# Fillers and a piecewise loop in the first transform, and new steps for pieces of batches one and two, in an FFT filter fused with a two-layer network

## The chip, the cores and the metric

The kernel runs on one core of one Trainium2 chip. The metric is device time in microseconds (us), the median of several executions. Every profile shown is one execution taken by the hardware profiler. In it PE is TensorE's matmul row, PEld its weight loads, DVE is VectorE, ACT is ScalarE, POOL is GpSimd and SP is SyncE; a "q" behind an engine's name means its sequencer or its DMA queue.

## The reference

```python
X = np.fft.rfft(x, axis=1)                  # x: (8, 3008, 256)
F = (filt_r + 1j * filt_i)[None, :, :]      # (1505, 256)
y = np.fft.irfft(X * F, n=3008, axis=1)     # global filter per channel
h = y.reshape(24064, 256) @ w_in            # (256, 2048)
g = np.maximum(h, 0) + alpha * np.minimum(h, 0)
out = g @ w_out                             # (2048, 256)
```

Eight batches are filtered along the sequence in the frequency domain, and each filtered row goes through a two-layer network with a leaky activation (one slope for each hidden unit).

## The kernel before

All matmuls are in fp16 with fp32 sums in PSUM. The order of all work is written out by hand: each engine executes its instructions in the order in which the program issues them.

**The transform.** A length of 3008 is 94 x 32. One transform has four stages. `piece_a` is the transform over the 94 (eight pieces). Its result is turned, so that the 32 lie on partitions: for batches 1 to 7 through memory (`save_a` writes `a_dram`, `turn_a` reads it back, both from SP's queue), for batch 0 on TensorE (`turn_at`, a matmul against the identity `id16`). `piece_b` is the transform over the 32 for some frequencies, into PSUM; VectorE multiplies what it gives by the filter (lines 186, 187, and 301 for batch 0). `piece_c` goes back over the 32, `keep_c` or an eviction stores it as `v`, and it is turned again (`turn_c` with `v_dram` and `zt`; for batch 0 `half_t` and `piece_t` on TensorE). The last stage, `half_d` or `pair_d`, goes back over the 94 and evicts into `yT`, the network's input.

**The first transform** (batch 0, class `First`) stands ahead of everything else. Until its first quarter is in `yT`, the network can't start. Its loop over `kp` (12 pairs of frequencies) runs two `piece_b`, two `piece_c`, one `keep_c` on ScalarE for both and one `turn_at`. In its waits `warm(n, kind)` puts n fillers: matmuls of `id16` against a broadcast of itself, 512 columns each, whose results nobody reads.

**The network** is cut into 48 blocks of 512 or 384 rows, and each block into 16 steps. In a step `up(j)` makes 128 hidden units of the block (two matmuls, line 457, into `hps`; ScalarE and VectorE activate into `gtb`), and `down(j)` does a sixteenth of the second layer of the block before (line 488, into `op`). A step has a number from 0 to 767. The transforms of batches 1 to 7 run as pieces put at fixed steps, by `plan_fft(b, a_at, ta, quarters, x_at, b_at, add, c_at, d_at)`: steps of the eight `piece_a`, of `turn_a`, of the loads of the next batch's x, of the six `piece_b`, `piece_c` and the eight `pair_d`.

**PSUM** has eight banks: `psH` two tiles of two banks (`hps`: `up`, `piece_a`, `piece_c`, and `piece_b` of batch 0), `psO` two tiles of one bank (`op`: `down`, fillers, `piece_c` of batch 0), and `psF` a single tile of two banks. `psF` is shared by `piece_b` of batches 1 to 7, whose tile VectorE reads twice, and by `pair_d`, whose tile ScalarE reads once. Whoever comes next on `psF` waits until the readers of the one before are done.

The code around the change, as it was:

Of the kernel before, what the change touches and what calls it, by code (L numbers as in the profile page):

```python
# [50 lines left out]
def kernel(  # L51
# [57 lines left out]
    def load_x(b, c):  # L109
        xs = p_x.tile([N1, 8 * D], FP16, name="xs")  # L110
        for r in (slice(0, 48), slice(48, N1)) :
            nc.gpsimd.dma_start(out=xs[r], in_=xrow(b, c)[r])  # L112
        return xs
# [13 lines left out]
    def banks(wide):  # L127
        if wide:
            return psH.tile([128, 2, 512], FP32, name="hps")
        return psF.tile([128, 2, 512], FP32, name="psF")  # L130

    def bank(kind):
        if kind == "o":
            return psO.tile([128, 2, D], FP32, name="op").rearrange("p k d -> p (k d)")
        return banks(kind == "h")[:, 0]


    class Fft:
# [61 lines left out]
        def piece_c(self, q):  # L200
            if q == 0:
                self.v = p_fft.tile([128, NK, D], FP16, name="v")
                self.zt = p_fft.tile([96, N2, D], FP16, name="zt")
            u, _ = self.uw.pop(q)
            ps = psH.tile([128, 2, 512], FP32, name="hps")
            for h in range(2):
                for e in range(2):
                    r = slice(64 * e, 64 * e + 64)
                    for par in range(2):
                        nc.tensor.matmul(ps[64 * par : 64 * par + 64, e, 256 * h : 256 * h + 256],  # L210
                                         twi_s[r, 4 * q + 2 * h + par], u[r, par, h], start=True, stop=True)
            on_act(self.v[:, 4 * q : 4 * q + 4].rearrange("p (h e) d -> p e h d", e=2),
                   ps.rearrange("p e (h d) -> p e h d", h=2))
# [19 lines left out]
                                 wi3_s, start=True, stop=True)  # L233
            return ps

        def half_d(self, i, evict, kind):
            g, dh, mh = i // 4, (i // 2) % 2, i % 2
            ps = self.inverse(bank(kind), g, dh, mh)
            t0 = self.base + g * NX
            evict(yT[:, dh, t0 : t0 + NX].rearrange("p (x m) -> p x m", m=8)[:, :, 4 * mh : 4 * mh + 4],  # L240
                  ps.rearrange("p m x -> p x m"))
# [16 lines left out]
    both = (on_act, on_dve)  # L258


    class First(Fft):
# [42 lines left out]
        def piece_c(self, kp):  # L304
            if kp % 2 == 0:
                self.ops = [psO.tile([128, 2, D], FP32, name="op") for _ in range(2)]
            u = self.uw.pop(kp)
            tw, tx = (t.rearrange("p k (c g e) -> p k g c e", c=2, e=4) for t in (twi_s, twx_s))
            for par in range(2):
                for f in range(2):  # L310
                    for i, t in enumerate((tw, tx)):
                        for e in range(2):
                            r = slice(64 * e, 64 * e + 64)
                            o = self.ops[e][:, kp % 2].rearrange("p (g w) -> p g w", g=16)
                            o = o[:, 8 * f : 8 * f + 8, 8 * par : 8 * par + 8]
                            nc.tensor.matmul(o.rearrange("p g (c e) -> p g c e", c=2),  # L316
                                             u[r, par, i, 128 * f : 128 * f + 128], t[r, 2 * kp + par],
                                             start=(i == 0), stop=(i == 1))

        def keep_c(self, kp, evicts):  # L320
            vm = self.vm.rearrange("p (g q k e) -> p g q k e", q=4, k=NK, e=4)
            for e in range(2):
                k = 2 * kp + e
                evicts[e](vm[:, :, :, k : k + 3 : 2], self.ops[e].rearrange("p k (g q e) -> p g q k e", q=4, e=4))

        def turn(self, pt, i, n):
            m = self.vm.rearrange("p (g m e) -> p g m e", m=96, e=4)
# [20 lines left out]
    def tables(eng, names, ka, kb):  # L348
        for n, t in (("twf", twf_s), ("twi", twi_s), ("twx", twx_s)):
            if n in names:  # L350
                eng.dma_start(out=t[:, ka:kb], in_=consts[n].ap()[:, ka:kb])

    xc = {(0, c): load_x(0, c) for c in range(4)}
    f0 = First()
# [14 lines left out]
    for c in range(4):  # L369
        xc[(1, c)] = load_x(1, c)  # L370

    def warm(n, kind="o"):
        pw = bank(kind)
        for _ in range(n):
            nc.tensor.matmul(pw.rearrange("p (r c) -> p r c", r=4), id16,
                             id16.unsqueeze(1).to_broadcast([128, 4, 128]), start=True, stop=True)

    warm(9)
    for i in range(8):
        f0.piece_a(i, both[i % 2], i % 3 < 2)  # L380
        if i % 2 == 1:
            warm((4, 2, 2, 2)[i // 2])
        if i == 5:
            nc.vector.memset(twf_s[:, 8:24, 0:1], 0.0)
            tables(nc.sync, ("twf", "twi", "twx"), 8, 24)
            nc.sync.dma_start(out=wi3_s, in_=consts["wi3"].ap())
            nc.sync.dma_start(out=wf1_s, in_=consts["wf1"].ap())
            nc.sync.dma_start(out=sgn_s, in_=sgn_d.ap())
            alp = psO.tile([128, 2, D], FP32, name="op")
            nc.tensor.transpose(alp[:, 0, 0:16], al16, id32)  # L390
            nc.vector.tensor_copy(al_s, alp[:, 0, 0:16])
            nc.vector.tensor_scalar(alm_s, al_s, 1.0, -1.0, OP.mult, OP.add)
    f0.turn_at(0, 1, on_act)
    f0.turn_at(1, 1, on_dve, True)
    f0.piece_b(0)
    f0.turn_at(2, 2, on_act)
    f0.piece_b(1)
    f0.turn_at(4, 2, on_act)
    for kp in range(0, 12, 2):
        if kp < 10:  # L400
            f0.piece_b(kp + 2)
            f0.piece_b(kp + 3)
        f0.piece_c(kp)
        f0.piece_c(kp + 1)
        f0.keep_c(kp, both if kp == 10 else (on_act, on_act))
        if kp < 6:
            f0.turn_at(kp + 6, 2, on_act)
        elif kp < 10:
            warm(1, "f")
    nc.gpsimd.dma_start(out=filt_s[:, 0:1], in_=f0.fst)  # L410
    for o in range(0, 128, 64):
        for i in range(0, 64, 32):
            nc.gpsimd.dma_start(out=filts_s[o + i : o + i + 32], in_=filt_s[o + 32 : o + 64])
    for o in (32, 96):
        nc.gpsimd.dma_start(out=filt_s[o : o + 32], in_=filt_s[o - 32 : o])
    warm(2, "f")
    for i, (evict, kind) in enumerate(((on_act, "o"), (on_dve, "o"), (on_act, "f"), (on_dve, "h"))):
        f0.half_t(i, evict, kind)
    warm(4)
    for i, evict, kind in ((0, on_act, "h"), (2, on_dve, "o"), (1, on_act, "o"), (3, on_dve, "f")):  # L420
        f0.half_d(i, evict, kind)


    sizes = [512] * 5 + [384] + [512] * 6
# [74 lines left out]
    def put(step, fn, *args):  # L499
        plan.setdefault(step, []).append((fn, args))  # L500

    def plan_fft(b, a_at, ta, quarters, x_at, b_at, add, c_at, d_at):
        f = Fft(b)
        for i in range(8):
            put(a_at[i], f.piece_a, i)
            front.add(a_at[i])
        for c in range(4):
            put(a_at[2 * c + 1], f.save_a, c)
            if b + 1 < NB:
                put(x_at[c],  # L510
                    lambda b=b, c=c: xc.update({(b + 1, c): load_x(b + 1, c)}))
        for q in range(quarters):
            w = NK // quarters
            put(ta, f.turn_a, nc.sync, w * q, w * q + w)
        for q in range(6):
            put(b_at[q], f.piece_b, q, not add)
            if add:
                put(b_at[q] + add, f.piece_s, q)
        for q in range(6):
            put(c_at[q], f.piece_c, q)  # L520
            front.add(c_at[q])
            if q % 2 == 1:
                put(c_at[q] + 1, f.turn_c, q // 2)
        for i in range(8):
            put(d_at[i], f.pair_d, i, on_act)
# [15 lines left out]
    def d_steps(p):  # L541
        return [p + t for t in (91, 93, 104, 108, 116, 120, 140, 152)]

    plan_fft(1, range(12, 28, 2), 28, 4, (17, 21, 25, 29), range(36, 72, 6), 0, range(48, 84, 6),
             (91, 93, 98, 101, 106, 116, 136, 152))
    plan_fft(2, (50, 56, 62, 68, 74, 80, 84, 88), 92, 4, (57, 69, 81, 89), (104, 114, 126, 136, 148, 158), 7,
             (114, 126, 136, 148, 158, 170), d_steps(96))
    for b in range(3, NB):
        p = 96 * (b - 1)
# [54 lines left out]
```

## Time and profile before

| | us |
|---|---|
| median of 3 executions | 793.56 (792.51 to 794.36) |
| profiled execution: time | 792.9 |
| profiled execution: span, first to last instruction | 791.1 |
| TensorE busy in the span | 768.3 (97%) |
| VectorE, ScalarE, GpSimd busy | 596.7, 582.9, 142.9 |
| mean granted TensorE clock | 0.989 of full speed |
| first matmul of step 0 | at 42.09 |

How to read the rows below: times are from the start of the span. A row of the timeline has the start, the time from the first to the last of its instructions, engine, line, operation, tile written and tiles read, shape, count, and in brackets how long the engine had been idle and what ended that. A row of the windows has the stretch, its length, busy time and count of each engine (PE, PEld, DVE, ACT, POOL), the granted TensorE clock, the mean share of DMA engines in use and GB/s. A matmul's record lasts longer than the time that it keeps the next one from starting: 273 ns for 256 columns of line 488, where the next starts 109 ns later.

### The profile page before, as it was taken

How to read it: one execution, taken by the hardware profiler on the slowest of the kernel's cores; microseconds unless marked ns; L12 is line 12 of the kernel's file. 1: busy time of each engine (PE TensorE's matmuls, PEld its weight loads, DVE VectorE, ACT ScalarE, POOL GpSimd, SP SyncE). 2: the span in 40 equal slices, each digit the busy share in tenths (PEclk: the TensorE clock that was granted, in tenths of full speed). 3: DMA queues.
4: the chain of work that ended last, by engine and by line, in shares of the span. 5: the costliest groups of instructions: out<-in, count | busy, mean ns of one | idle time of the engine just before them, and what ended most of it. 6: DMA issues, size and time to landing. Idle time of an engine off the chain costs nothing.

```text
span 791.1 us, 16237 instructions
## 1 busy us (share of the span) xinstructions
PE 768.3 (97%) x6428; PEld 512.9 (65%) x6428; DVE 596.7 (75%) x1117; ACT 582.9 (74%) x669; POOL 142.9 (18%) x271
## 2 busy tenths in 40 slices
PE   6889999899999999999999999999999999999997
PEld 3556666566666666766666666766666666766665
DVE  2776985677868788788877878687877888766663
ACT  2678688777777887698767887788866777677664
POOL 6521461022202220022101221010100111000000
PEclk8799999999999999999999999999999999999999
DMA  9987698746683566546493655934474233511112
GB/s 196 173 197 168 134 175 177 202 111 142 148 192 84 134 156 122 159 95 165 107 193 100 139 113 142 205 79 110 104 151 127 55 94 85 149 42 27 41 41 54
DMA packets 95084, 100.66 MB, mean 127 GB/s; under 512 B 11280, under 2 KB 82464, under 8 KB 94816
## 3 DMA queue, kind: packets, MB, share of 16 engines
q1 hardware_dynamic: 80368, 70.25, 34.0%
q0 software_dynamic: 14640, 29.38, 21.5%
q8 instruction: 50, 0.82, 0.4%
q14 instruction: 26, 0.21, 0.1%
HBM read 55.28 MB, written 46.66 MB: 129 GB/s over the span
## 4 chain that ended last, share of the span: by engine, by line
PE 90%; ACT 3%; DMA 2%; DVE 2%; issue 1%; SPq 1%; POOL 1%; DVEq 0%; ACTq 0%; POOLq 0%
PE hps L457 40%; PE op L488 40%; PE hps L155 3%; PE psF L232 2%; PE psF L179 2%; ACT gtb L466 2%; PE hps L210 1%; DMA xs<-in_x_dram 1%; DMA filt_s<-in_filt_r_dram 1%; DVE uu L301 1%; SPq L168 1%; ACT asb L253 1%; POOL xs L112 0%; PE op L316 0%; PE psF L332 0%
## 5 line engine op out<-in xcount | busy, mean ns | idle before, releaser
L466 ACT ACTIVATE gtb<-hps 128x1024 f16<-128x1024 f32 (+1 forms) x384 | 385.6, 1005 | 137.8 <-PE hps L457 136.8
L457 PE MATMUL hps<-yT,win_s 128*128 128x512 f16 (+1 forms) x1536 | 435.1, 375 | 2.0 <-ACT gtb L466 1.5
L488 PE MATMUL op<-wout_s,gtb 128*128 128x256 f16 x3008 | 435.8, 273 | 0.1
L488 PEld LDWEIGHTS <-gtb 128*128 128x128 f16 x3008 | 294.0, 98 | 168.3 <-issue 0.4
L469 DVE TENSOR_SCALAR m<-gtb,alm_s 128x512 f16<-128x512 f16 (+1 forms) x768 | 233.0, 346 | 154.0 <-ACT gtb L466 153.1
L471 DVE TENSOR_TENSOR gtb<-gtb,m 128x2048 f16<-128x2048 f16 (+1 forms) x192 | 231.0, 1203 | 10.1
L457 PEld LDWEIGHTS <-win_s 128*128 128x128 f16 x1536 | 142.6, 98 | 60.1 <-issue 15.4
L193 POOL DMA_DIRECT2D sw<-ww x144 | 70.8, 500 | 385.1 <-DVE ww L186 382.3
L253 ACT ACTIVATE asb<-hps 96x1024 f16<-96x1024 f32 x56 | 57.1, 1019 | 11.7 <-PE hps L155 11.4
L493 ACT ACTIVATE osb<-op 128x512 f32<-128x512 f32 (+1 forms) x97 | 56.2, 579 | 5.3 <-issue 2.8
L253 ACT ACTIVATE v<-hps 128x1024 f16<-128x1024 f32 x42 | 43.0, 1024 | 15.1 <-PE hps L210 15.1
L253 ACT ACTIVATE yT<-psF 128x752 f16<-128x752 f32 x58 | 46.3, 798 | 10.2 <-PE psF L232 10.1
L112 POOL DMA_DIRECT2D xs<-in_x_dram x64 | 36.4, 611 | 96.1 <-PE hps L155 84.9
L186 DVE TENSOR_TENSOR ww<-psF,filts_s 128x1024 f16<-128x1024 f32 x42 | 51.1, 1217 | 0.0
L187 DVE TENSOR_TENSOR uu<-psF,filt_s 128x1024 f16<-128x1024 f32 x42 | 51.0, 1214 | 0.0
L232 PEld LDWEIGHTS <-zt 96*128 96x128 f16 x512 | 28.9, 99 | 8.4 <-issue 3.2
L155 PE MATMUL hps<-xs,wf_s 94*96 94x512 f16 x112 | 33.4, 379 | 0.2 <-ACT gtb L466 0.2
L232 PE MATMUL psF<-wi_s,zt 96*128 96x94 f16 x484 | 30.2, 205 | 3.2 <-DVE uu L187 3.1
L198 DVE TENSOR_TENSOR uu<-uu,sw 128x1024 f16<-128x1024 f16 x36 | 24.6, 684 | 0.0
L191 POOL DMA_DIRECT2D uu<-ww x24 | 19.3, 1221 | 26.2 <-DVE uu L187 21.9
L179 PE MATMUL psF<-at,twf_s 64*64 64x256 f16 x336 | 17.8, 281 | 2.4 <-DMA at<-a_dram 1.3
L210 PE MATMUL hps<-uu,twi_s 64*64 64x256 f16 x336 | 16.5, 271 | 0.0
(60 smaller groups left out, 171.5 us busy)
## 6 DMA issues: line engine op xcount, KB each, us to landing
out_dram<-osb SPq DMA_DIRECT2D x160, 128.0 KB
a_dram<-asb SPq DMA_DIRECT2D x28, 384.0 KB
v_dram<-v SPq DMA_DIRECT2D x84, 128.0 KB
zt<-v_dram SPq DMA_DIRECT2D x28, 384.0 KB
sw<-ww POOLq DMA_DIRECT2D x144, 64.0 KB, 2.5
at<-a_dram SPq DMA_DIRECT2D x20, 384.0 KB
xs<-in_x_dram POOLq DMA_DIRECT2D x32, 192.0 KB, 4.1
xs<-in_x_dram POOLq DMA_DIRECT2D x32, 184.0 KB, 5.8
```

Source lines behind the costliest of these rows:

```text
L155: nc.tensor.matmul(ps[0:96, u], wf1_s, xs[:, o : o + 512], start=True, stop=True)
L186: nc.vector.tensor_mul(ww, px, fs)
L187: nc.vector.tensor_mul(uu, px, f)
L193: nc.gpsimd.dma_start(out=sw[o : o + 32], in_=ww[i : i + 32])
L232: nc.tensor.matmul(ps[:, m], self.zt[:, 8 * g + 4 * mh + m, dh * 128 : dh * 128 + 128], wi3_s, start=True, stop=True)
L253: nc.scalar.activation(o, i, AF.Copy)
L457: nc.tensor.matmul(self.hps[:, j % 2, 0:tn], win_s[:, kt, j * 128 : (j + 1) * 128], yT[:, kt, self.t0 : self.t0 + tn], start=(kt == 0), st ...
L466: nc.scalar.activation(g[:, 2 * i : 2 * i + 2], self.hps[:, :, 0:tn], AF.Copy)
L469: nc.vector.tensor_scalar(m[:, 2 * i + h], g[:, 2 * i + h], 0.0, a, OP.min, OP.mult)
L471: nc.vector.tensor_add(g, g, m)
L488: nc.tensor.matmul(self.op[:, si - s0], self.gts[k][:, 128 * si : 128 * si + 128], wout_s[:, k], start=(si == s0 and k == 0), stop=(si == ...
L493: nc.scalar.activation(osb[:, 0:m], self.op[:, 0:m], AF.Copy)
```

## The change

In the first transform the fillers change in number and place, the loop over `kp` takes one `piece_b` and one `piece_c` at a time, the last `piece_c` writes into `psF` and the last two are evicted one by one. In the plan, four of batch 1's `pair_d` get later steps, batch 2's last two `piece_a` and its `turn_a` get earlier ones, and the load of one piece of batch 3's x goes with them. Nothing that is computed changes.

```diff
-        def half_d(self, i, evict, kind):
+        def half_d(self, i, evict, kind, fill=0):
             g, dh, mh = i // 4, (i // 2) % 2, i % 2
-            ps = self.inverse(bank(kind), g, dh, mh)
+            pd = bank(kind)
+            warm(fill, pd)
+            ps = self.inverse(pd, g, dh, mh)
...
         def piece_c(self, kp):
...
+            if kp == 11:
+                pf = banks(False)
+                warm(5, pf[:, 0])
+                self.ops = [pf[:, e].rearrange("p (k d) -> p k d", k=2) for e in range(2)]
+            kb = 0 if kp == 11 else kp % 2
...
-        def keep_c(self, kp, evicts):
+        def keep_c(self, kp, evicts, n=2):
...
-            warm((4, 2, 2, 2)[i // 2])
+            warm((4, 4, 8, 3)[i // 2], bank("o"))
...
     f0.turn_at(0, 1, on_act)
     f0.turn_at(1, 1, on_dve, True)
+    warm(2, bank("o"))
     f0.piece_b(0)
     f0.turn_at(2, 2, on_act)
     f0.piece_b(1)
+    warm(2, bank("o"))
     f0.turn_at(4, 2, on_act)
-    for kp in range(0, 12, 2):
+    for kp in range(12):
         if kp < 10:
             f0.piece_b(kp + 2)
-            f0.piece_b(kp + 3)
         f0.piece_c(kp)
-        f0.piece_c(kp + 1)
-        f0.keep_c(kp, both if kp == 10 else (on_act, on_act))
-        if kp < 6:
-            f0.turn_at(kp + 6, 2, on_act)
-        elif kp < 10:
-            warm(1, "f")
+        if kp > 9:
+            f0.keep_c(kp, (on_act, on_act) if kp == 10 else both, 1)
+        elif kp % 2 == 1:
+            f0.keep_c(kp - 1, (on_act, on_act))
+            if kp < 7:
+                f0.turn_at(kp + 5, 2, on_act)
+        if 7 <= kp < 10:
+            warm(2, banks(False)[:, 0])
...
-    warm(2, "f")
+    warm(4, bank("h"))
     for i, (evict, kind) in enumerate(((on_act, "o"), (on_dve, "o"), (on_act, "f"), (on_dve, "h"))):
         f0.half_t(i, evict, kind)
-    warm(4)
-    for i, evict, kind in ((0, on_act, "h"), (2, on_dve, "o"), (1, on_act, "o"), (3, on_dve, "f")):
-        f0.half_d(i, evict, kind)
+    for i, evict, kind, fill in ((0, on_act, "h", 1), (2, on_dve, "o", 0), (1, on_act, "o", 1), (3, on_dve, "f", 0)):
+        f0.half_d(i, evict, kind, fill)
...
     plan_fft(1, range(12, 28, 2), 28, 4, (17, 21, 25, 29), range(36, 72, 6), 0, range(48, 84, 6),
-             (91, 93, 98, 101, 106, 116, 136, 152))
-    plan_fft(2, (50, 56, 62, 68, 74, 80, 84, 88), 92, 4, (57, 69, 81, 89), (104, 114, 126, 136, 148, 158), 7,
+             (91, 93, 98, 101, 110, 120, 142, 154))
+    plan_fft(2, (50, 56, 62, 68, 74, 80, 82, 84), 90, 4, (57, 69, 81, 85), (104, 114, 126, 136, 148, 158), 7,
              (114, 126, 136, 148, 158, 170), d_steps(96))
```

More of the change, by code (lines that the diff above doesn't have):

```diff
@@ L313, in piece_c @@
                             r = slice(64 * e, 64 * e + 64)
-                            o = self.ops[e][:, kp % 2].rearrange("p (g w) -> p g w", g=16)
+                            o = self.ops[e][:, kb].rearrange("p (g w) -> p g w", g=16)
                             o = o[:, 8 * f : 8 * f + 8, 8 * par : 8 * par + 8]
@@ L323, in keep_c @@
                 k = 2 * kp + e
-                evicts[e](vm[:, :, :, k : k + 3 : 2], self.ops[e].rearrange("p k (g q e) -> p g q k e", q=4, e=4))
+                evicts[e](vm[:, :, :, k : k + 2 * n - 1 : 2],
+                          self.ops[e][:, 0:n].rearrange("p k (g q e) -> p g q k e", q=4, e=4))
         def turn(self, pt, i, n):
@@ L370, with warm @@
         xc[(1, c)] = load_x(1, c)
-    def warm(n, kind="o"):
-        pw = bank(kind)
+    def warm(n, pw):
         for _ in range(n):
@@ L376, in warm @@
                              id16.unsqueeze(1).to_broadcast([128, 4, 128]), start=True, stop=True)
-    warm(9)
+    warm(9, bank("o"))
     for i in range(8):
```

## The prediction

> **What bounds the kernel now.** I read the page's shares first, then its chain, then the windows of the first 60 us, the timeline of the first transform, and last TensorE's idle rows behind it.
>
> ```profile
> PE 90%; ACT 3%; DMA 2%; DVE 2%; issue 1%; SPq 1%; POOL 1%; DVEq 0%; ACTq 0%; POOLq 0%
> PEclk8799999999999999999999999999999999999999
> ```
>
> TensorE carries 90% of the chain, so time is won only where it waits or runs slowly. The clock is short of full in the first two slices alone. The windows show when (PE's busy time and, third from the end, the clock):
>
> ```profile
> 3.50:6.91 3.41, 3.41 (x16) 1.41 (x15) 0.00 (x0) 0.00 (x0) 2.99 (x6) 1.00 1.05 202
> 10.33:13.74 3.41, 1.48 (x19) 0.81 (x18) 1.80 (x3) 1.09 (x2) 1.59 (x4) 1.00 1.10 233
> 13.74:17.15 3.41, 2.66 (x21) 1.77 (x22) 1.31 (x3) 0.81 (x1) 3.41 (x7) 0.50 1.15 295
> 30.81:34.22 3.41, 1.93 (x66) 1.13 (x66) 3.27 (x3) 1.27 (x3) 0.54 (x1) 1.00 1.36 192
> 37.63:41.05 3.42, 3.42 (x25) 2.30 (x24) 1.37 (x2) 1.31 (x3) 1.11 (x2) 0.50 1.08 212
> 47.87:51.29 3.42, 2.45 (x14) 0.99 (x12) 3.38 (x9) 2.57 (x4) 0.43 (x1) 1.00 0.86 187
> ```
>
> The clock changes only at multiples of 3.41 us. It falls to half at 13.74 and 34.22, each time after a stretch with PE busy 1.48 or 1.93 of 3.41; it stays full after 2.45. It returns at 23.98 and 41.05. So 17 us run at half clock, in the one part where the network can't start.
>
> ```profile
> 20.49 1.22 DVE L301 TENSOR_TENSOR uu<-hps,filt_s 128x1024 f16<-128x1024 f32 x1 [0.30 <-DMA filt_s<-in_filt_r_dram]
> 22.61 11.47 DVE L301 TENSOR_TENSOR uu<-hps,filt_s 128x1024 f16<-128x1024 f32 x10 [0.90 <-PE hps L297]
> 33.52 0.19 PE L316 MATMUL op<-gtb,uu 64*128 64x64 f16 x1 [0.79 <-issue]
> 38.59 1.91 PE L375 MATMUL op<-id 128*128 128x512 f16 x4
> 40.30 0.52 PE L232 MATMUL hps<-wi_s,zt 96*128 96x94 f16 x4
> 42.09 0.59 PE L457 MATMUL hps<-yT,win_s 128*128 128x512 f16 x2
> ```
>
> The middle of the transform (22.61 to 34.08) is VectorE's: ten products, one after the other. Behind it come transposes and fillers at half clock until step 0 at 42.09.
>
> ```profile
> 147.35 0.30 PE L179 MATMUL psF<-at,twf_s 64*64 64x256 f16 x2 [0.70 <-DMA at<-a_dram]
> 148.26 0.41 PE L179 MATMUL psF<-at,twf_s 64*64 64x256 f16 x6 [0.61 <-DMA at<-a_dram]
> 151.77 0.49 PE L232 MATMUL psF<-wi_s,zt 96*128 96x94 f16 x8 [1.15 <-DVE uu L187]
> 154.05 0.59 PE L457 MATMUL hps<-yT,win_s 128*128 128x512 f16 x2 [0.16 <-ACT asb L253]
> 163.09 0.51 PE L232 MATMUL psF<-wi_s,zt 96*128 96x94 f16 x8 [1.19 <-DVE uu L187]
> 185.23 0.41 PE L179 MATMUL psF<-at,twf_s 64*64 64x256 f16 x8 [1.08 <-ACT yT L253]
> 201.73 0.49 PE L232 MATMUL psF<-wi_s,zt 96*128 96x94 f16 x8 [0.71 <-DVE uu L187]
> ```
>
> These are all of TensorE's idle rows from 71 to 240 us. Four are `psF`: `pair_d` at steps 106, 116 and 152 waits for VectorE to read `piece_b`'s tile, and at 136 `piece_b` waits for `pair_d`'s eviction. Two are the turned data of batch 2 coming late to step 104.
>
> **The change, part one: the first transform.** I walk TensorE's path at full clock. A filler of 512 columns costs 0.216 us at full and 0.427 at half clock (start to start), a transpose of 128 columns 0.056 or 0.107.
>
> Does the clock stay full? In 10.33 to 13.74 eight fillers come in (2 after piece 3, 6 after piece 5): 1.48 + 8 x 0.216 = 3.2 busy, above 2.45. The stretch up to 17.15 holds 16 matmuls (0.85), 3 fillers (0.65), eight transposes (0.64 with their drain) and one more filler: 2.35, the tightest. In 30.81 to 34.22, 1.93 plus some five fillers is 2.9. Between 1.93 and 2.45 the trace tells nothing; I take full clock throughout.
>
> [...]
>
> Start: the alpha transpose still waits for its DMA until 14.21, and eight fillers from 11.89 end at 13.6, so they are hidden. Pieces 6 and 7, the two small `turn_at`, `piece_b(0)` and `turn_at(2)` go at full clock, with five added fillers; `piece_b(2)` comes at 20.1 instead of 21.91. VectorE's second product still waits for its filter rows (20.4). The third starts at 21.6 instead of 22.61, but the fifth needs a filter load whose last semaphore VectorE saw at 23.92: it starts at 24.0 instead of 24.94. Gain on VectorE's row: 0.94.
>
> The loop gives some of it back. A pair of products takes 2.27 us. In the new order a `piece_c` pair with a `piece_b` between costs 0.23 + 0.32 + 0.23 plus two switches of 0.09; then drain and semaphores 0.25, the two ScalarE evictions 1.09 and a semaphore 0.06 before `op` is free again: 2.36 a round. So `psO` takes VectorE's place, by 0.1 a pair, and the two fillers between `piece_c(8)` and `piece_b(11)` add 0.4. I get the release of `op` for `piece_c(10)` at 33.6; before it was 34.99, after the 0.95 "issue" stall (0.79 idle and 0.16 drain). Whether this stall, whose cause the trace doesn't show, comes again is open: 0 to 0.95; I take 0.
>
> From there: `piece_c(10)` 0.25, five fillers 1.08, `piece_c(11)` 0.25, then four fillers 0.86, which cover its eviction: transposes from 36.1, where it was 36.88. The eight real transposes take 0.92 instead of 1.71 (gain 0.79). The four fillers at 38.59 kept `half_d` from data that was there by 38.7; with one filler and the wait for two evictions 0.48 remains of 1.71 (gain 1.23). The `half_d` themselves gain 0.14. Step 0 is earlier by 0.78 + 0.79 + 1.23 + 0.14 = **2.9 us**. The 15.07 us of steps 0 to 15 are ScalarE's and keep their length; win_s and wout_s have landed by 38.3, GpSimd's queue is unchanged in order, and its filts_s copies (landed at 53.3) are first used on VectorE at step 16, near 54.3, so they still fit.
>
> **Part two: batches one and two.** To each idle I add the drain of 0.16 that the matmul's record hides. Steps 110, 120, 142 and 154 lie 4 to 6 steps behind the last `piece_b` and at least 4 ahead of the next. A step is 0.87 us or more; two products are 2.4. So none should wait: 1.31 + 1.35 + 1.25 + 0.87 = **4.8 us**. At step 106 `pair_d` also met batch 3's first `piece_a`; the following 0.16 idle (0.3 with drain) goes too.
>
> The turned data: SP is free at 136.1, and with `piece_a(7)` at step 84 instead of 88 the last `save_a` goes there directly instead of at 138.81, behind the stores of step 87. The wait for its landing then ends some 2.7 us sooner. The first quarter now arrives by 148.2, so it comes at 145.5 to 146.5; step 104 asks for it at 146.4. Of 0.86 + 0.80 I count **1.5**. Stores behind `turn_a` on SP move forward with it, so ScalarE isn't held at `osb`. The price: three `piece_a` two steps apart in the 384-row block, where ScalarE needs 0.70 + 0.91 and a share of `osb`, about what TensorE needs (1.73): 0 to 0.6, by the rows there (0.18 to 0.27 after each piece) I take 0.3. The x load at step 85 moves by four steps to a slot freed at 84, beside the loads of `zt`: 0 to 2 if `zt` came late to step 91; no idle shows there now, so 0. Sum: 4.8 + 0.3 + 1.5 - 0.3 = **6.3 us**.
>
> TensorE shows hardly an idle after 202 us, and all of it hangs on its own order, so both gains last to the end: 9.2 us. On the profiled execution 792.9 becomes 783.7; on the median, 0.66 above it, 784.4.
>
> **The rivals.**
> - The clock falls once more (the stretch at 13.74 or at 34.22 counts too little, or the stretches begin elsewhere). At 34.22 fillers and transposes double: 9 fillers 1.9 more, eight transposes 0.8, less what evictions hide: gain 0.6 instead of 2.9, **786.7**. Against it: 2.35 and 2.9 lie nearer to 2.45 than to 1.93.
> - The stalls of part two turn into others: ScalarE is busy 45.6 us of 140 to 200, and would be 45.6 of 53.7 (85%) without them; or the data is still late for 104. If half comes back, gain 6.1, **787.5**. Against it: 60 to 80 us has ScalarE busy 17.0 of 20 with TensorE idle only 0.5.
> - Slower: the fillers are dead weight. If matmuls against the identity don't count as activity, the clock stays at half from the first transform to step 16. Then 14 added fillers and slow pieces delay step 0: `piece_b(2)` +1.2, a loop of 2.5 to 3.4 a pair to 37.4 for `piece_c(10)`, then 2.1 + 0.9 + 0.6 + 1.2 to the transposes at 42.1 (+5.2), and steps 0 to 15, with up pairs of 0.86, cost 4 more (each its own 0.43 twice, less ScalarE's waits that this hides). So 5.2 + 4.0 lost, 6.3 won in part two: +2.9, **796.5**. It decides once step 16 starts more than 6.3 us later than 57.16. Against it: at 6.91 the clock rose after a stretch of nothing but fillers. [...]
> - It does nothing: the plan's moves are visible in each queue's order, so only a gain eaten whole would do.
>
> **How the numbers follow.** Forecast 0.72, clock 0.12, given back 0.10, dead weight 0.04, nothing 0.02. The forecast's own range is 782.0 (the clock and a faster loop, 2.4 more) to 786 ("issue" stall and a late turn). Reaching to the next two cases: 782.0 to 788.0. Faster by over 0.2% (1.6 us, about what a measurement of this kernel can tell from no change) 0.94, same 0.02, slower 0.04.
>
> **What would show it.** Right: clock 1.00 in every stretch from 6.91 on, step 0 near 39.2, no idle before line 232 or 179 between 100 and 220, and the rest of the profile unchanged but shifted. Wrong: a spell of 0.50 behind 13.74 or 34.22; new idle before line 457 that ends on ScalarE in 120 to 200; line 179 still waiting for `at`.

## The result and the profile after

The kernel after takes 788.1 us (median of 6 executions, 785.52 to 788.5) where the kernel before takes 793.18 in the same comparison (6 executions, 792.19 to 794.36). The ratio is 0.9931, interval 0.9915 to 0.9947: 5.1 us are gained by the medians and 5.5 by the ratio, of the 9.2 that the sum gave. The profiled execution took 788.27 us with a span of 786.5.

Three lines of the page of the kernel after follow: the granted clock and the share of DMA engines in use over 40 slices of the span, and the chain by engine. The fence behind them has the DMA row of the kernel before.

```profile
PEclk9999999999999999999999999999999999999999
DMA  9978688756664657555593655834474233511112
...
PE 88%; DMA 8%; POOL 1%; ACT 1%; DVE 1%; issue 1%; SPq 0%; ACTq 0%; POOLq 0%
```

```profile
DMA  9987698746683566546493655934474233511112
```

DMA has 8% of the chain instead of 2%. The first four slices (0 to 79 us) have DMA engines busy 70% to 90% and more, as they had before; the prediction did not read that row. The longest transfers of the chain up to step 36 show where DMA came in (start, length, what):

```profile
27.26 15.45 DMA xs<-in_x_dram
...
43.03 6.11 DMA filt_s<-fst
...
50.97 8.46 DMA filts_s<-filt_s
...
70.60 7.00 DMA a_dram<-asb
...
79.05 2.17 DMA at<-a_dram
```

The loads of batch 1's x, the copies behind them in GpSimd's queue (`fst`, `filts_s`), the last `save_a` and the reading back decide when step 36 starts. In this chain no instruction of TensorE stands ahead of 64.34 us, while in the kernel before it ran through VectorE's products and TensorE from 23.78 us on. By this chain a faster TensorE ahead of 64 us would not have shortened the kernel any further.

Where the time went is best read from the first `up` matmul of a few steps (line 457 before, 466 after):

| step | before, us | after, us | difference |
|---|---|---|---|
| 0 | 42.09 | 41.29 | -0.80 |
| 24 | 66.87 | 66.41 | -0.46 |
| 36 | 80.36 | 81.60 | +1.24 |
| 80 | 125.81 | 127.05 | +1.24 |
| 104 | 148.60 | 148.59 | -0.01 |
| 116 | 163.43 | 160.48 | -2.95 |
| 136 | 185.79 | 181.69 | -4.10 |
| 152 | 202.05 | 197.09 | -4.96 |
| 767 | 778.86 | 774.23 | -4.63 |

So the stretch that holds the moved pieces (steps 80 to 767) gained 5.9 us, close to the 6.3 of the sum; the first transform gained 0.8 instead of 2.9 by step 0, and by step 36 that had turned into a loss.

The windows of the kernel after around the place where its clock fell (columns as in the prediction):

```profile
30.71:34.12 3.41, 1.69 (x43) 0.95 (x42) 1.77 (x2) 1.08 (x2) 0.53 (x2) 1.00 1.28 192
34.12:37.54 3.42, 3.42 (x33) 1.33 (x26) 0.02 (x1) 1.04 (x3) 0.52 (x1) 0.50 1.44 208
```

PE is busy only 1.69 us of the first stretch, less than the 1.93 that let the clock fall before, and the next stretch runs at half. The early spell (13.74 to 23.98 before) is gone, as forecast; this later one is shorter than it was (3.42 us instead of 6.83), but it is there. What TensorE did there stands in its timeline and in VectorE's:

```profile
31.98 0.38 PE L299 MATMUL hps<-at,twf_s 64*32 64x256 f16 x9 [1.27 <-issue]
...
34.20 2.32 PE L382 MATMUL psF<-id 128*128 128x512 f16 x5
```

```profile
32.40 1.23 DVE L303 TENSOR_TENSOR uu<-hps,filt_s 128x1024 f16<-128x1024 f32 x1 [1.14 <-PE hps L299]
```

TensorE stops for 1.27 us in the middle of `piece_b(11)`, with nothing that the profile shows to wait for. This is the "issue" stall of before (0.79, then in the middle of a `piece_c`) at another place and longer. VectorE's last product waits 1.14 for it, and the five fillers, now at half clock, take 2.1 us start to start instead of 1.08 (the row's 2.32 has the tail of the last record).

TensorE's idle rows of the kernel after from 71 to 240 us, all of them:

```profile
80.40 0.30 PE L179 MATMUL psF<-at,twf_s 64*64 64x256 f16 x2 [0.93 <-DMA at<-a_dram]
81.26 0.41 PE L179 MATMUL psF<-at,twf_s 64*64 64x256 f16 x6 [0.56 <-DMA at<-a_dram]
148.26 0.41 PE L179 MATMUL psF<-at,twf_s 64*64 64x256 f16 x6 [0.30 <-DMA at<-a_dram]
```

Every row of line 232 that the prediction showed (1.15, 1.19, 0.71), and the row of line 179 at 185.23, are gone. The turned data of batch 2 at step 104 still comes 0.30 late, and a new pair of rows stands at step 36: the turned data of batch 1 is late there by 0.93 and 0.56.

### The profile page after: what moved, and what is told of

Its sections match the earlier page's. It is cut to its first block, busy times and chain, and to the rows that moved or that the text cites. A ratio compares the mean times of both kernels' runs of the same rounds, so it can differ in the third digit from the quotient of the medians.

```text
span 786.5 us, 16280 instructions
## 1 busy us (share of the span) xinstructions
PE 770.0 (98%) x6450; PEld 512.1 (65%) x6450; DVE 596.2 (76%) x1117; ACT 583.0 (74%) x671; POOL 142.3 (18%) x271
## 4 chain that ended last, share of the span: by engine, by line
PE 88%; DMA 8%; POOL 1%; ACT 1%; DVE 1%; issue 1%; SPq 0%; ACTq 0%; POOLq 0%
PE op L497 40%; PE hps L466 40%; DMA xs<-in_x_dram 3%; PE hps L155 3%; PE psF L232 2%; DMA a_dram<-asb 2%; PE psF L179 2%; PE hps L210 1%; DMA filts_s<-filt_s 1%; DMA filt_s<-fst 1%; DMA filt_s<-in_filt_r_dram 1%; POOL filt_s L122 1%; DMA at<-a_dram 1%; POOL xs L112 0%; ACT gtb L475 0%
```

## The experiments

### The two halves, and the four moved pieces alone

**plan_only** is the kernel before with the new steps of `plan_fft`:

```diff
-             (91, 93, 98, 101, 106, 116, 136, 152))
-    plan_fft(2, (50, 56, 62, 68, 74, 80, 84, 88), 92, 4, (57, 69, 81, 89), ...
+             (91, 93, 98, 101, 110, 120, 142, 154))
+    plan_fft(2, (50, 56, 62, 68, 74, 80, 82, 84), 90, 4, (57, 69, 81, 85), ...
```

> The kernel before with the new step numbers alone; the first transform is the old one. Theory A (the four waits on psF and the late turned data are simply gone): between step 80 and step 160 the trace of the change gained 5.9 us, so the time is 5.5 to 6.5 us below the kernel before, ratio 0.992, and no idle over 0.3 us stands before lines 232 and 179 from 100 to 220 us. Theory B (these stalls come back elsewhere when step 0 is where it was, or part of the gain came only since the first transform had moved everything): under 4 us.

**fft_only** is the kernel after with the old steps put back.

> The changed first transform with the old step numbers. Theory A (what the profile of the change shows is the rule: TensorE stops at its 961st recorded instruction for over a microsecond, the clock falls once at 34, and the data for step 36 comes late): step 0 is 0.5 to 1 us earlier, step 36 loses 1 to 2, and the time is within 1.5 us of the kernel before. Theory B (the profiled execution was a bad one; the sum on record holds): 2.9 us faster, ratio 0.9963.

**pairs_only**, run later, is the kernel before with only the first of the two changed lines: four `pair_d` of batch 1 at 110, 120, 142 and 154.

> The kernel before with one edit: batch 1's pair_d at steps 110, 120, 142, 154 instead of 106, 116, 136, 152. By the sum on record 4.8 us and the 0.3 of step 106: 788.2. The change's plan as a whole gave 5.0 to 5.5 on the chip; if the pairs alone give that, the earlier piece_a and turn_a of batch 2 are worth nothing or cost what they win (theory F); if they give 4 or less, those earlier steps earn about 1 (theory A).

Measured, each against the kernel before on the same chip:

| kernel | median, us | before, us | ratio (interval) |
|---|---|---|---|
| plan_only | 787.97 | 792.98 | 0.9933 (0.9919 to 0.9948) |
| fft_only | 793.13 | 792.98 | 1.0003 (0.9993 to 1.0012) |
| pairs_only | 787.43 | 792.92 | 0.9933 (0.9918 to 0.9949) |

The new first transform alone, among these loads, is worth nothing: its interval is -0.6 to +1.0 us. The four `pair_d` alone bring the whole gain, 5.3 us by the ratio, where the sum had 4.8 and 0.3; batch 2's earlier `piece_a` and `turn_a` add nothing to that which the medians show. The traces say the same of the four: from step 104 to step 152, nine of the ten profiles with the moved pieces take 48.50 us (late_loads, below, 49.29), and the four with the old ones 53.26 to 54.34. TensorE's idle rows of pairs_only at step 104:

```profile
146.76 0.30 PE L179 MATMUL psF<-at,twf_s 64*64 64x256 f16 x2 [0.37 <-DMA at<-a_dram]
147.60 0.41 PE L179 MATMUL psF<-at,twf_s 64*64 64x256 f16 x6 [0.55 <-DMA at<-a_dram]
```

Without the earlier `turn_a`, 0.92 of idle is left there; with it, 0.30 in the kernel after and 0.66 in its second profile (after_again, below). But fft_only, without it, has 0.51, so the gain here is small. Elsewhere the earlier pieces can lose more: TensorE's one large idle row in plan_only (whose profiled execution, 792.18 us, was the slowest of its seven) is

```profile
139.14 0.51 PE L232 MATMUL psF<-wi_s,zt 96*128 96x94 f16 x8 [3.43 <-DMA zt<-v_dram]
```

at step 91: the `zt` of batch 1 came late, by 3.43 us. A wait for `zt` there also stands in the profiles of five later kernels that have the earlier pieces (late_loads, x_later, neg_later, all_later, old_fft_late: 0.75 to 2.95 us), though not in the two of the kernel after nor in that of late_all, and in none of the five kernels without them (before, fft_only, pairs_only, old_all_later, old_late_all). That the earlier `save_a` of batch 2 delays the `zt` transfer fits this, but no run moved it alone.

### The kernel after once more

**after_again** is the kernel after, unchanged, to see how its first transform varies between executions.

> The changed kernel itself once more, for a second trace. Theory A: the stop at the 961st recorded TensorE instruction (1.0 to 1.6 us), the spell of half clock behind it and the wait of 1 to 2 us for the turned data at step 36 are there again; 788. Theory B (accidents of one execution): at least two of the three are missing in this trace.

It gave 788.31 us, ratio 0.9939 (0.9925 to 0.9953). In its profile the stop was only 0.39 us (start to start; 1.55 in the other execution), the clock did not fall before 80 us, and step 0 came at 38.70, earlier than the 39.2 forecast. Of the 2.6 us that this is ahead of the other execution 0.8 were left at step 36 (80.82 against 81.60) and none at step 104 (149.26 against 148.59); the two executions took 788.97 and 788.27 us. The first fence is VectorE's timeline of this execution, the second TensorE's idle rows:

```profile
57.63 0.62 DVE L545 TENSOR_SCALAR filts_s<-filts_s,sgn_s 128x1536 f16<-128x1536 f16 x1 [1.99 <-DMA filts_s<-filt_s]
```

```profile
62.53 0.49 PE L232 MATMUL psF<-wi_s,zt 96*128 96x94 f16 x8 [1.29 <-DVE yT L258]
...
79.27 0.30 PE L179 MATMUL psF<-at,twf_s 64*64 64x256 f16 x2 [1.61 <-DMA at<-a_dram]
80.25 0.64 PE L179 MATMUL psF<-at,twf_s 64*64 64x256 f16 x6 [0.68 <-DMA at<-a_dram]
```

Two transfers take the gain back. VectorE's sign change of `filts_s`, put at step 16, waits 1.99 us for the copies to land, and with it the eviction that TensorE waits for at 62.53. At step 36 the turned data of batch 1 is late by 1.61 and 0.68. An earlier step 0 only makes these waits longer.

### Loads held back

**late_loads** asks whether the stop comes from the loads beside the first transform. The loads of `win_s`, `wout_s` and batch 1's x (four transfers of 512 KB, four of 192 and four of 184, 3.6 MB) are issued ahead of the loop; here they wait for VectorE's eighth product (to 27.44 us), by a memset that it then writes into `win_s`:

```diff
-    for kt in range(2):
-        nc.gpsimd.dma_start(out=win_s[:, kt], ...)
-    ...                                  # wout_s, load_x(1, 0..3)
     for kp in range(12):
...
+        if kp == 5:
+            nc.vector.memset(win_s[:, :, 0:1], 0.0)
+            ...                          # the same loads
```

> The changed kernel with the loads of w_in, w_out and batch 1's x held back until VectorE's eighth product (a memset on w_in's tile that the first of them must wait for). Theory A (the stop at the 961st instruction is TensorE's instruction fetch waiting behind these loads): the stop shrinks under 0.3 us, the clock stays full, and step 0 comes 1.5 to 2.5 us earlier than in the change (at 39 to 39.8 instead of 41.3); what follows on the loads, filts_s and step 36, gets no better. Theory B (the fetch is slow by itself, or is asked for too late): the stop stays at 1.0 to 1.6 us.

It gave 790.43 us, ratio 0.9965 (0.9952 to 0.9978): slower than the kernel after. Yet the stop was gone, the clock stayed full up to 52.83 us and step 0 came at 38.36, even earlier than theory A had it. TensorE's idle rows tell where the gain went:

```profile
51.14 0.59 PE L155 MATMUL hps<-xs,wf_s 94*96 94x512 f16 x2 [1.62 <-ACT asb L255]
64.97 0.49 PE L232 MATMUL psF<-wi_s,zt 96*128 96x94 f16 x8 [1.51 <-DVE yT L258]
...
80.99 0.30 PE L179 MATMUL psF<-at,twf_s 64*64 64x256 f16 x2 [0.88 <-DMA at<-a_dram]
```

The loads now stand ahead of the `fst` and `filts_s` copies in GpSimd's queue. The `fst` copy went at 43.67 instead of 39.76; `asb` shares its buffer, so batch 1's first `piece_a` waited 1.62. The sign change waited 2.83, until 60.08. By step 36 all was lost again (82.35).

What the stop is: TensorE stops after the same count of recorded instructions in every kernel with the early loads, 961 (953 matmuls and weight loads and 8 of the sequencer), whatever comes next (a `piece_c` before, a `piece_b` after). Among the DMA queues on the page of the kernel after (packets, MB, share) stands

```profile
q8 instruction: 50, 0.82, 0.4%
```

These are 50 packets of 16,384 bytes, one to some 258 of TensorE's 12,900 instructions; no other engine has a tenth as many. The third packet began at 29.72 us in the kernel after, when 937 instructions had started, and TensorE went on at 31.98. In all ten profiles with the early loads it began when 877 to 961 had started, and TensorE went on 2.25 to 2.51 us after that. In the four with the loads held back (late_loads and three kernels further on) it began when 746 to 762 had started (in late_loads at 26.53), and nothing stopped. So TensorE's own program came late where these loads stood beside it. The trace doesn't show what a packet waited for.

### Later users of the transfers

**x_later**: batch 2's x is loaded at later steps, so that it does not lie beside the last `save_a` of batch 1.

```diff
-    plan_fft(1, range(12, 28, 2), 28, 4, (17, 21, 25, 29), ...
+    plan_fft(1, range(12, 28, 2), 28, 4, (37, 43, 51, 63), ...
```

> The changed kernel with one edit: the loads of batch 2's x go from steps 17, 21, 25, 29 to 37, 43, 51, 63, behind the turning of batch 1's data. Theory D (the transfers of the first 77 us set step 36, whatever the first transform does: these 1.5 MB share the DMA engines with the last write to a_dram and its reading back): the write lands in under 6 us instead of 7.0 to 7.8, the waits of 1.8 to 2.6 us before line 179 at step 36 shrink by over 1 us, and the time falls by 1 to 2 us against the change (786.5). Theory E (step 36 waits for something else, such as SP's queue or the write itself): the waits stay and the time is that of the change, 788.2.

**neg_later**: the sign change is put ten steps later.

```diff
-        put(16 + 2 * i, neg, 3 * i, 3 * i + 3)
+        put(26 + 2 * i, neg, 3 * i, 3 * i + 3)
```

> The changed kernel with one edit: VectorE's four sign products on filts_s go from steps 16, 18, 20, 22 to 26, 28, 30, 32. Theory D: VectorE no longer waits near 56 us for the copies into filts_s, the 0.7 to 1.5 us lost before line 232 near 63 us is gone, but step 36 still waits for the turned data until the same time, so the total changes by less than 0.7 us against the change. Theory E (the first transform's gain is lost at step 16 to 24): 1 to 1.5 us faster than the change.

**all_later**: both, and two x loads of batch 3 at 97 and 101 instead of 81 and 85.

> The changed kernel with both edits, and the loads of the last two pieces of batch 3's x at steps 97 and 101 instead of 81 and 85 (away from the reading of zt). Theory D: nothing holds TensorE back by clock time any more, so the first transform's 0.8 to 3.4 us reach the end: 3 us below the change, near 785, ratio to the kernel before 0.989 to 0.991. Theory E: within 1 us of the change.

**old_all_later**: the same three edits in the kernel before (batch 3's loads from 81 and 89).

> The control: the kernel before with the same later loads and sign products, without the change. Theory D: before, step 36 came just in time for its data, so taking the transfers out of its way gives 0 to 0.7 us and the time stays within 1 us of the kernel before (792 to 793.5). If it gains 2 us or more, the gain of the kernel above is that of the later loads and not the first transform's.

| kernel | median, us | ratio to before, 793.49 (interval) | step 0 | step 36 |
|---|---|---|---|---|
| x_later | 788.07 | 0.9937 (0.9919 to 0.9954) | 43.55 | 81.69 |
| neg_later | 787.54 | 0.9934 (0.9917 to 0.9951) | 40.46 | 80.70 |
| all_later | 787.94 | 0.9933 (0.9910 to 0.9956) | 41.67 | 79.46 |
| old_all_later | 793.07 | 1.0002 (0.9987 to 1.0017) | 41.03 | 78.80 |

Each edit removes the wait that it is aimed at. The landing of the last `save_a` of batch 1 in SP's timeline, the kernel before first, then the kernel after, then x_later (the second row starts when the write has landed):

```profile
71.05 0.31 SPq L161 DMA_DIRECT2D a_dram<-asb  x1
76.39 3.71 SPq L168 DMA_DIRECT2D at<-a_dram  x8
```

```profile
70.60 0.31 SPq L161 DMA_DIRECT2D a_dram<-asb  x1
77.71 2.27 SPq L168 DMA_DIRECT2D at<-a_dram  x5
```

```profile
72.54 0.32 SPq L161 DMA_DIRECT2D a_dram<-asb  x1
75.62 4.67 SPq L168 DMA_DIRECT2D at<-a_dram  x10
```

The write takes 5.3 us before, 7.1 in the kernel after and 3.1 in x_later, where the mean share of DMA engines in use from 60 to 77 us is 0.39 instead of 0.91. So in the kernel after the data came 1.3 us later than before, although the write was issued 0.45 earlier. No wait at step 36 is left in x_later; in neg_later the wait near 63 us is gone. But the time moves in none of the four. In x_later's profile, the slowest of its six executions (790.19), the start was lost (full clock only from 11.75 us, a stop of 2.10, a half-clock spell at 35.64), and new waits came at 125.89 (0.80, `piece_c`'s `uu` late by DMA) and 138.41 (0.75, `zt`). In all_later step 36 was 2.1 us earlier than in the kernel after, and this was lost again by step 104 (149.16 against 148.59): `uu` was 0.62 late and `zt` 1.35, although the x loads of steps 81 and 85 had been moved away, so these two loads alone are not the cause of the late `zt`.

### Everything out of the way

**late_all** is all_later with the loads held back as in late_loads, but in the order of need: the `fst` copy, `win_s`, `wout_s`, half of batch 1's x, the `filts_s` copies, the other half.

```diff
+        if kp == 5:
+            nc.vector.memset(win_s[:, :, 0:1], 0.0)
+            nc.gpsimd.dma_start(out=filt_s[:, 0:1], in_=f0.fst)
+            ...                          # win_s, wout_s, load_x(1, 0..1)
+            ...                          # the four filts_s copies
+            ...                          # load_x(1, 2..3)
```

> The changed kernel with the later loads and sign products of the runs before, and the loads of w_in, w_out and batch 1's x again held back until VectorE's eighth product, this time with the copy of the first filter rows ahead of them and the copies into filts_s among them, so that neither waits for the last of x. Theory D (part one's gain is there, but transfers take it: first TensorE's instruction fetch, then the data of steps 16 and 36): no stop at the 961st instruction, step 0 at 38 to 39, no wait at steps 12 to 36 over the 0.84 us that the kernel before has there, step 36 at 76 to 77.5 instead of 80.4; the time is 783 to 785, ratio 0.987 to 0.990. Theory E (something else gives the gain back): 786.5 or more.

**old_late_all** is the kernel before with the same held-back loads and later steps; neither the new transform nor the moved pieces.

> The control: the kernel before, without the change, with the same held-back loads and later steps. Theory D: without the stop at the 961st instruction (0.95 to 1.3 us) the old first transform reaches step 0 near 41, still with its two spells of half clock, and that gain now lasts: 791 to 792.5. So the changed transform is worth 2 to 3 us where transfers leave it alone. Theory E (the held-back loads are the gain, and the fillers and the loop are worth nothing): step 0 at 39 or earlier here too, 789 or less.

**old_fft_late** is late_all with the old first transform: it has the moved pieces.

> The old first transform with everything else of the fastest kernel so far (held-back loads, later steps, the change's plan). What the changed transform is worth where transfers leave it alone is this kernel's time less 784.7. Theory D1 (the fillers still pay: the old transform keeps one or two spells of half clock, as its granted clock of 0.991 to 0.996 in most runs says): 786 to 787.5, ratio 0.991 to 0.993. Theory D2 (once the fetch isn't held up, the old transform is as good; its best profile had step 0 at 38.6 against 38.1): 785.3 or less, ratio 0.990 or less.

| kernel | first transform | moved pieces | median, us | before, us | ratio (interval) | step 0 | step 36 |
|---|---|---|---|---|---|---|---|
| late_all | new | yes | 784.71 | 792.92 | 0.9891 (0.9877 to 0.9906) | 38.09 | 75.88 |
| old_fft_late | old | yes | 785.15 | 793.40 | 0.9895 (0.9875 to 0.9916) | 39.33 | 77.10 |
| old_late_all | old | no | 791.68 | 792.92 | 0.9982 (0.9971 to 0.9994) | 38.63 | 76.40 |

The profiled executions of the two kernels with the old transform were off their medians: old_fft_late's was its slowest (788.79), old_late_all's its fastest (788.97).

late_all is the fastest kernel of all: 8.6 us below the kernel before by its ratio, where the kernel after is some 5 below it (0.9931 and 0.9939). TensorE's timeline of it, step 0 and the longest idle row behind it:

```profile
38.09 0.61 PE L470 MATMUL hps<-yT,win_s 128*128 128x512 f16 x2
...
143.28 0.41 PE L179 MATMUL psF<-at,twf_s 64*64 64x256 f16 x6 [0.84 <-DMA at<-a_dram]
```

No stop, full clock from 7.69 us to the end of the work, and an early step 0 that lasts. But the control shows whose merit that is. Step 0 in old_late_all and old_fft_late:

```profile
38.63 0.59 PE L461 MATMUL hps<-yT,win_s 128*128 128x512 f16 x2
```

```profile
39.33 0.59 PE L461 MATMUL hps<-yT,win_s 128*128 128x512 f16 x2
```

I had expected old_late_all near 41, with the old transform's half-clock spells. One spell stayed (16.50 to 23.33), but the one behind 34 us was gone with the stop, and in these two kernels step 0 came within 0.5 to 1.2 us of late_all's. So where nothing holds the program up, the new transform is worth some 0.5 to 1.2 us at step 0, one profile each; by the medians late_all and old_fft_late can't be told apart (0.9891 and 0.9895), with intervals that leave room for 2 us either way. The later and reordered transfers and the later sign change together are worth the rest: 0.9933 (plan_only, pairs_only) against 0.9895, some 3 us. No run has the order of the loads alone. With the old pieces the same edits bring only 1.4 us in the median (theory D's range, though step 0 came as early as theory E said), and 4.0 in the profiled execution (step 767 at 774.91 against 778.86). Why the other executions of old_late_all (up to 794.17) lost that again is open: they have no trace, only mean clocks of 0.991 to 0.996.

## Why the prediction was right and wrong

The measured 788.1 lies 2.1 above the forecast's own range (782 to 786) and just past the end of the wider one (788.0). It comes near the 787.5 of the second rival, but by luck: there half of part two came back, and here part two's moved `pair_d` came whole and part one was lost.

**Right: the four moved `pair_d`.** 4.8 + 0.3 forecast, 5.3 measured (pairs_only), and nothing new became late behind them: in the kernel after and in pairs_only line 232 has no idle row between 100 and 220 us. The rival of stalls that turn into others did not come for these.

The 15.07 us of steps 0 to 15, forecast to stay, are 15.09.

**Wrong in size: the turned data, 1.5 less 0.3.** On the medians nothing of it shows (plan_only and pairs_only are both 0.9933), though 1.2 us is 0.0015, no more than the intervals leave open. The step that failed is that the wait for the landing "then ends some 2.7 us sooner". The last `save_a` did go directly, at 136.91 us in the kernel after instead of 138.81, but right behind the one before it (135.82), and `turn_a` began 7.7 us later, at 144.62, where before it began 5.7 later, at 144.53. Step 80 lay 1.24 us later by then, so a little was won: from step 80 to step 104 the two profiles of the kernel after take 21.54 and 21.73 us, the five with the old pieces 21.91 to 22.99. But the other seven with the new pieces take 21.88 to 26.01. The price that was set aside ("0 to 2 if `zt` came late to step 91; no idle shows there now, so 0") did come, 0.75 to 3.43 us in the six profiles that show it.

**Wrong: that the first transform is 2.9 us shorter for the whole kernel.** The walk to step 0 was sound where nothing disturbed it: step 0 at 38.70 in after_again, 38.36 in late_loads, against 39.2 forecast. But the kernel before pays for the stop too: with the loads held back the old transform reaches step 0 at 38.63 and 39.33, so only 0.5 to 1.2 of the 2.9 us are the new transform's own. Three steps failed.
- "Whether this stall, whose cause the trace doesn't show, comes again is open: 0 to 0.95; I take 0." It comes in all kernels with early loads, 0.39 to 2.88 us from the start of the 961st instruction to that of the 962nd, the most in plan_only (before 0.98, after 1.55). It stands at one instruction count, and the new order of work did not take it away. In the kernel after and in x_later, neg_later and all_later the clock fell to half behind it; in fft_only the stop of 1.83 lay across two stretches (PE busy 2.46 and 2.20 of 3.41) and the clock stayed up. Gain at step 0 in the kernel after: 0.80.
- "... its filts_s copies (landed at 53.3) are first used on VectorE at step 16, near 54.3, so they still fit." VectorE waited 1.21 us for them in the kernel after, and 1.99, until 57.63, in after_again.
- "... all of it hangs on its own order, so both gains last to the end." Up to step 36 it hangs on transfers. With batch 2's x loads at steps 17 to 29, step 36 lies at 80.1 to 82.4 in all eight profiles, whether step 0 was at 38.36 (late_loads, 82.35) or at 42.09 (before, 80.36). A wait at step 36 that is hidden before appears when TensorE gets there earlier or the data later. The row of DMA shares of the kernel before (9987 at the start) was the warning.

**One reading** of the prediction was off without moving its sum. The stretch up to 6.91 us held fillers until 6.28 and matmuls of `piece_a` behind them, so it is not of fillers alone.

**The rivals.** The clock did fall once more in the profiled execution, as the first rival said, with step 0 2.1 us later than forecast; but fft_only, whose clock stayed full from 8.2 us, gained nothing either, so that is not where the time went. The fillers are not dead weight: all six profiles with the old transform have a spell of half clock that begins between 13.35 and 16.75 us, and none of the eight with the new fillers has one before 31.82. Nothing came out slower.

## What to carry to other kernels

Before adding up gains ahead of a fixed point, ask what arrives there by the clock: loads, copies and turned data whose issue does not move along make a wall, and an earlier engine only waits longer at it (here step 36 at 80.36 with step 0 at 42.09, and at 80.82 with step 0 at 38.70). Read the DMA row slice by slice, not only the chain, which names a transfer only once TensorE waits for it. An "issue" idle at the same instruction count in two versions of a kernel (here behind the 961st, in the kernel before and in the kernel after) is hardly an accident of the order of work: look at the queue of instruction packets and at what is loaded beside it, then order the loads by need. And compare a change with the old code under the same repaired conditions, as old_fft_late does here, before crediting the change with a gain.

## What the runs showed of the hardware

- **TensorE's program came in by DMA packets while it ran, and came late beside the early loads.** The queue that the page of the kernel after calls `instruction` moved 50 packets, 0.82 MB; that they are TensorE's is read from the counts above. The stop after 961 TensorE instructions lasted 0.39 to 2.88 us in the ten profiles with 3.6 MB of loads issued ahead of the loop, and was 0 in the four with these loads held back. That the late packet is the cause is read from its time (TensorE went on 2.25 to 2.51 us after the packet began, ten times of ten) and from that; no run changed the program's length alone.
- **A write to memory took longer beside loads.** The last `save_a` of batch 1 (384 KB) landed in 3.1 us in all six profiles without x loads beside it, and in 5.3 to 7.8 in the eight with them.
- **The clock changed at other times in each execution.** It first rose to full at 5.75 to 11.75 us (6.91 in the kernel before, where fillers started 0.43 us apart up to 6.28 and 0.22 apart from 7.25), and changed from then on only at multiples of 3.41 us from that rise. In the kernel after it fell at 34.12, behind a stretch whose longest idle was 1.27 us.
- **The clock fell behind stretches with little work.** Counted in steps of 3.41 us from the first rise, every fall before 60 us in the fourteen profiles came behind a stretch with PE busy 0.86 to 1.99 us, and none behind more. Two stretches with 1.95 and 1.96 stayed up, so PE's busy time by the records does not tell the falls from the rest on its own.
